# Pooled attention and an affine residual MLP on one core: the first batch's start put in another order

## Chip, core and metric

The kernel runs on one core of a Trainium2 chip. The metric is the device time of one execution in microseconds (us), lower is better. Before the change three executions took 361.34, 361.68 and 361.83 us, median 361.68. The profiled execution has a span of 360.4 us.

## What is computed

Two stages in one kernel. The first is attention over pooled keys and values: 8 batches, 8 heads, 576 tokens, 64 features a head. k and v are averaged over groups of 8 tokens, so that there are 72 keys a head. The second is a residual block: mixing over tokens with a 576x576 matrix, then a two-layer MLP with 2048 hidden columns. All inputs and the output are float32.

```python
k_p = k.reshape(B, H, Sp, 8, D).mean(axis=3)          # Sp = 72
v_p = v.reshape(B, H, Sp, 8, D).mean(axis=3)
attn = softmax(scale * q @ k_p^T)                      # over the 72 pooled keys
x = (attn @ v_p), heads side by side                   # (8, 576, 512)

a1 = alpha1 * x + beta1
tok = einsum('ts,bsd->btd', w_tok, a1)
u = x + lam * tok
a2 = alpha2 * u + beta2
ch = relu(a2 @ w_ch1) @ w_ch2
out = u + lam * ch
```

Setup work is done once in the kernel: `lam` and `lam * alpha1` are spread over 128 partitions (a product of a row of ones with the vector), w_tok is transposed and its row sums are appended, beta2's share is folded into a bias of the hidden columns, and w_ch2 is multiplied by lam.

## The kernel before

Each engine takes its instructions in program order. Tokens are split: rows 0 to 511 of a batch in a main part, rows 512 to 575 as the remainder ("rem"). Loads that change the type to 16 bits go through GpSimd's queue, the others through the sync or the scalar queue. The pieces of attention of one batch are functions which the program calls in an order of its own:

```python
def broadcast(i, out, by=None):                # vector i to all partitions
    ps = gp("ps_bc")
    nc.tensor.matmul(out=ps, lhsT=ones_row, rhs=vecs[0:1, i])      # float32
    if by is None:
        nc.scalar.copy(out=out, in_=ps)
    else:
        nc.vector.tensor_tensor(out=out, in0=by, in1=ps, op=ALU.mult)

def keep_warm(count):                          # products that nothing reads
    ps = psB.tile([P, DM], FP, tag="ch", bufs=2, name="ps_warm")
    for _ in range(count):
        nc.tensor.matmul(out=ps, lhsT=warm[:, 0:P], rhs=warm)

# att_F(b, hp): 4 transposes of q of two heads on TensorE, then a copy to qT
# att_Frem(b):  2 transposes of the remainder of q, then a copy
# att_K(b, u):  pools k of four heads on TensorE, copies to kpT (half on ScalarE, half on VectorE)
# first_V(b, u): pools v of four heads: 6 products, 2 copies
# att_S(b, h):  scores of a head (3 products), 2 exponentials on ScalarE -> ET
# att_AV(b, h): 5 products of ET with pooled v, reciprocal and normalisation on VectorE -> x
# att_X(b, h0, h1, eng): xs = x * lam * alpha1 for heads h0 to h1
# mix_T(b, c):  token mixing of one chunk of 128 tokens: 5 products, u = x + ..., u_bf = u * alpha2
# mix_uT(key):  4 transposes of u_bf, copy to u_fm on ScalarE
# setup_wtok(t): 5 transposes of w_tok's tile t, copy;  setup_rowsum(t): 5 products, copy
# setup_bias(g): 16 narrow products for the bias of 4 hidden tiles, copy
# mlp_A(n, j):  hidden tile j of block n: 4 products, activation -> Hj
# mlp_B(n, m, part): a quarter of the second layer for chunk m
# scale_w2(g):  w2[g] *= lam on VectorE (128 x 2048)
```

The PSUM tiles named `gp` share six buffers. The first batch is called in this order:

```python
new_batch(1)
keep_warm(2)
broadcast(1, lamal_bc)                         # alpha1
broadcast(0, lam_bc)                           # lam
keep_warm(1)
cast_rem(0, nc.vector)
bias_rows()                                    # two products beta1 * lam, one row each
att_F(0, 0)
att_F(0, 1)
att_Frem(0, nc.scalar.copy)
keep_warm(1)
att_K(0, 0, None)                              # its first lines copy k on VectorE
nc.vector.tensor_tensor(out=lamal_bc, in0=lamal_bc, in1=lam_bc, op=ALU.mult)
more_constants()
keep_warm(2)
att_S(0, 0)
att_S(0, 1)
# ... cut: att_F of heads 4 to 7, scores 2 to 5, second half of k, first half of v
att_AV(0, 0)
att_AV(0, 1)
# ... cut: the other heads, xs, tiles 0 to 3 of w_tok with their row sums
mix_T(0, 0, nc.gpsimd)
setup_rowsum(3)
mix_T(0, 1, nc.gpsimd)
# ... cut: loads of w1[3] and w2
mix_T(0, 2)
mix_T(0, 3)
mix_uT((0, 0))
mix_uT((0, 1))
setup_bias(0)
mlp_A(0, 0, 0, 256)
mix_uT((0, 2))
for j in range(1, 4):
    mlp_A(0, j, 0, 256)
mix_uT((0, 3))
for j in range(4):
    mlp_A(0, j, 256, 512)
```

After that a loop over 9 blocks of 512 tokens sorts the pieces by a number: hidden tile j of a block stands at j, the second layer from 16 on, and the attention of the next batch and the rest of the setup lie between.

```python
if n == 0:
    todo.append((4.6, lambda: setup_wtok(4, nc.scalar.copy)))
    todo.append((6.2, lambda: setup_rowsum(4)))
    todo.append((8.3, setup_wtok_odd))
    for g in range(1, 4):
        todo.append((4 * g - 0.8, lambda g=g: setup_bias(g)))
    for g in range(4):
        todo.append(((11.0, 11.2, 11.4, 16.6)[g], lambda g=g: scale_w2(g)))
```

Of the kernel before, what the change touches and what calls it, by code (L numbers as in the profile page):

```python
# [23 lines left out]
def kernel(  # L24
# [42 lines left out]
    def new_batch(b):  # L67
        st1[b] = {"qT": [None] * 2, "ET": [None] * H, "raw": [None] * 2, "q": [None] * 2,
                  "k": [None] * 2, "v": [None] * 2}
# [4 lines left out]
    def load_q_bf(b, u, behind=None):  # L74

        bf = work.tile([P, 4, 4, D], BF, tag="q_bf", bufs=4, name="q_bf")
        if behind is not None:
            behind.memset(bf[:, 0, 0, 0:1], 0.0)
        nc.gpsimd.dma_start(out=bf.rearrange("p h c d -> p h (c d)"), in_=rows(q, b, u))
        st1[b]["q"][u] = bf  # L80
# [36 lines left out]
    def load_rem(b, queue=nc.sync, behind=None):  # L117

        raw = work.tile([P, 2, 2, 2, D], FP, tag="rem_raw", bufs=2, name="rem_raw")
        if behind is not None:  # L120
            behind.memset(raw[:, :, :, 0, 0:1], 0.0)
        for i, src in enumerate((q, k)):
            for h in range(2):
                (nc.scalar if h and not b else queue).dma_start(
                    out=raw[:, i, h].rearrange("p c d -> p (c d)"),
                    in_=src[b, h::2, 512:576, :].rearrange("a (i c) d -> i a (c d)", c=2))
        st1[b]["rem_raw"] = raw
# [25 lines left out]
    def cast_rem_k(eng):  # L153
        raw, rk = st1[0]["rem_raw"], st1[0]["rem"][1]
        eng.tensor_copy(out=rk[:, :, 0:2], in_=raw[:, 1])
        eng.tensor_copy(out=rk[:, :, 2], in_=raw[:, 1, :, 0])
# [26 lines left out]
    ones_row = const.tile([1, P], FP, tag="ones_row", name="ones_row")  # L183
    nc.vector.memset(ones_row, 1.0)

    def load_vector(i, src):
        n = 65 if i in (0, 3) else 1
        nc.scalar.dma_start(out=vecs[0:n:64, i],
                            in_=src.unsqueeze(0).to_broadcast((1 + n // 65, DM)))

    new_batch(0)
    load_rem(0)
    load_q_bf(0, 0)
    load_k16(0, 0)
    load_vector(1, moe_alpha1)
    load_vector(0, moe_lam)
    start = const.tile([1, 2], FP, tag="start", name="start")
    nc.vector.memset(start, 0.0)
    nc.scalar.activation(out=start[:, 1:2], in_=start[:, 0:1], func=AF.Exp, bias=0.0, scale=1.0)
    load_vector(3, moe_beta1)  # L200
    nc.scalar.dma_start(out=b2row, in_=moe_beta2.rearrange("(c p) -> c p", p=P))
    warm = const.tile([P, DM], BF, tag="warm", name="warm")
    nc.vector.memset(warm, 0.0)
# [12 lines left out]
    each4 = pool_each.rearrange("p (g a) j -> p g a j", a=4)  # L216
    nc.gpsimd.affine_select(out=identity_bf, in_=identity_bf, compare_op=ALU.not_equal,
                            fill=1.0, base=0, pattern=[[-1, P]], channel_multiplier=1)
    load_q_bf(0, 1)
    nc.gpsimd.affine_select(out=identity, in_=identity, compare_op=ALU.not_equal,  # L220
                            fill=1.0, base=0, pattern=[[-1, P]], channel_multiplier=1)
    for t, n, width in ((pool_main, 64, 2),):
# [4 lines left out]
    nc.gpsimd.affine_select(out=each4, in_=each4, compare_op=ALU.not_equal, fill=0.125,  # L227
                            base=0, pattern=[[-16, 8], [-1, 4], [-4, 4]], channel_multiplier=1)
    load_k16(0, 1)
    load_v16(0)  # L230
    load_wtok()

    vp1_pool, kpT_pool, ET_pool = [], [], []
# [19 lines left out]
                            in1=pool_v[0:32, 1:16:2], op=ALU.add)  # L253
    nc.vector.tensor_reduce(out=pool_rem, in_=pool_each, op=ALU.max, axis=AX.X)

    def bias_rows():
        for i, p0 in ((0, 64), (1, 0)):
            nc.vector.tensor_tensor(out=xs_pool[i][p0:p0 + 1, 4, :], in0=vecs[p0:p0 + 1, 3],
                                    in1=vecs[p0:p0 + 1, 0], op=ALU.mult)

    b2c_bf = const.tile([P, 4], BF, tag="b2c_bf", name="b2c_bf")
    wtT = const.tile([P, 6, 640], BF, tag="wtT", name="wtT")
# [8 lines left out]
    def load_al2(behind):  # L271
        behind.memset(al2_bc[:, 0:1], 0.0)
        nc.sync.dma_start(out=al2_bc, in_=moe_alpha2.unsqueeze(0).to_broadcast((P, DM)))
# [102 lines left out]
    def att_Frem(b, copy=None):  # L376
# [11 lines left out]
                                identity=identity_bf)  # L388
        copy(out=st["rem_qT"], in_=ps_q[:, 0:256].rearrange("p (c t) -> p c t", c=2))

    def att_K(b, u, copy):

        st = st1[b]
        ps_kp = gp("ps_kp")
        kp = ps_kp[:, 0:4 * SPG].rearrange("p (h g) -> p h g", g=SPG)
        n, nr = (1, 1) if b else (4, 2)
        if not b:
            nc.vector.tensor_copy(out=st["k"][u][:, :, 4], in_=st["k"][u][:, :, 0])
            if u == 0:
                cast_rem_k(nc.vector)  # L400
        for h in range(4):
            for c in range(n):
                nc.tensor.matmul(  # L403
                    out=kp[:, h, 0:64],
                    lhsT=st["k"][u][:, h, c:c + 2].rearrange("p a d -> p (a d)"),
                    rhs=pool_main, start=(c == 0), stop=(c == n - 1))
        for hh in range(2):
            for c in range(nr):
                nc.tensor.matmul(  # L409
                    out=kp[:, hh:4:2, 64:72],  # L410
                    lhsT=st["rem"][1][:, hh, c:c + 2].rearrange("p a d -> p (a d)"),
                    rhs=pool_rem.rearrange("p (g u r) -> p u r g", r=2, u=2)[:, u],
                    start=(c == 0), stop=(c == nr - 1))
        for a in range(2):
            rows = slice(64 * a, 64 * a + 64)
            (copy or (nc.scalar.copy, nc.vector.tensor_copy)[a])(  # L416
                out=kpT_pool[u][rows, a], in_=kp[rows])
# [87 lines left out]
    def keep_warm(count):  # L505
# [4 lines that stand above are left out]
# [75 lines left out]


    new_batch(1)
    keep_warm(2)
    broadcast(1, lamal_bc)
    broadcast(0, lam_bc)  # L590
    keep_warm(1)
    cast_rem(0, nc.vector)
    bias_rows()
    att_F(0, 0)
    att_F(0, 1)
    att_Frem(0, nc.scalar.copy)
    keep_warm(1)
    att_K(0, 0, None)
    nc.vector.tensor_tensor(out=lamal_bc, in0=lamal_bc, in1=lam_bc, op=ALU.mult)
    more_constants()  # L600
    keep_warm(2)
    att_S(0, 0)
    att_S(0, 1)
    att_F(0, 2, nc.vector.tensor_copy)
    att_F(0, 3, nc.vector.tensor_copy)
    att_S(0, 2)
    keep_warm(1)
    att_K(0, 1, None)
    load_al2(nc.vector)
    att_S(0, 3)  # L610
    setup_vectors()
    keep_warm(1)
    att_S(0, 4)
    first_V(0, 0)
    att_S(0, 5)
    att_AV(0, 0)
    att_AV(0, 1)
    for g in range(2):
        load_w1(g)
    load_q_bf(1, 0)  # L620
    load_q_bf(1, 1)
    load_w1(2)
    att_X(0, 0, 2, nc.gpsimd)
    first_V(0, 1)
    att_S(0, 6)
    att_AV(0, 2)
    att_S(0, 7)
    att_AV(0, 3)
    load_rem(1, behind=nc.vector)
    att_X(0, 2, 4, nc.gpsimd)  # L630
    att_AV(0, 4)
    att_AV(0, 5)
    setup_wtok(0, nc.scalar.copy)
    att_X(0, 4, 6, nc.gpsimd)
    att_AV(0, 6)
    setup_wtok(1, nc.scalar.copy)
    att_AV(0, 7)
# [5 lines left out]
    setup_wtok(3, nc.scalar.copy)  # L643
    att_X(0, 6, 8)
    setup_rowsum(2)
    load_v16(1)
    keep_warm(1)
    mix_T(0, 0, nc.gpsimd)
    setup_rowsum(3)
    mix_T(0, 1, nc.gpsimd)  # L650
    load_w1(3)
    for g in range(3):
        load_w2(g)
    mix_T(0, 2)
    mix_T(0, 3)
    mix_uT((0, 0))
    mix_uT((0, 1))
    setup_bias(0)
    mlp_A(0, 0, 0, 256)
    mix_uT((0, 2))  # L660
    for j in range(1, 4):
        mlp_A(0, j, 0, 256)
    mix_uT((0, 3))
    for j in range(4):
        mlp_A(0, j, 256, 512)

# [52 lines left out]
    for n in range(NBLK):  # L719
        todo = []  # L720
        for j in range(0 if n else 4, NJ):
            todo.append((j, lambda j=j: mlp_A(n, j)))
        for m in range(4):
            for part in range(4):
                at = 16 + (4 * m + part if n else 4 * part + m)
                todo.append((at, lambda m=m, part=part: mlp_B(n, m, part)))
        if n == 0:
            todo.append((4.6, lambda: setup_wtok(4, nc.scalar.copy)))
            todo.append((6.2, lambda: setup_rowsum(4)))
            todo.append((8.3, setup_wtok_odd))  # L730
            for g in range(1, 4):
                todo.append((4 * g - 0.8, lambda g=g: setup_bias(g)))
            for g in range(4):
                todo.append(((11.0, 11.2, 11.4, 16.6)[g], lambda g=g: scale_w2(g)))
        b = n + 1
        if b < B:
            todo += attention(b)
            if b + 1 < B:
                new_batch(b + 1)
                gate = nc.vector if b == 1 else None  # L740
                for u in range(2):
                    at = 21.0 + 0.2 * u
                    todo.append((at, lambda b=b, u=u: load_k(b + 1, u, gate)))
                    at = {1: 21.0, 2: 7.2}.get(b, 0.4) + 0.1 * u
                    todo.append((at, lambda b=b, u=u: load_q_bf(
                        b + 1, u, nc.vector if b == 2 else None)))
                    at = 19.0 + 0.2 * u if b == 1 else 3.5 + 4.0 * u
                    todo.append((at, lambda b=b, u=u: load_v(b + 1, u, behind=gate)))
                todo.append((20.9, lambda b=b: load_rem(b + 1, behind=gate)))
        for _, do in sorted(todo, key=lambda x: x[0]):  # L750
            do()
# [30 lines left out]
```

The softmax here doesn't subtract the row's maximum and nothing guards it: scores larger than these inputs give would overflow.

## Time and profile before

| engine | busy us | share of the span |
|---|---|---|
| PE (TensorE products) | 345.3 | 96% |
| PEld (TensorE weight loads) | 186.7 | 52% |
| DVE (VectorE) | 209.5 | 58% |
| ACT (ScalarE) | 154.1 | 43% |
| POOL (GpSimd) | 86.6 | 24% |

DMA moved 44.58 MB. The profile's second part cuts the span into 40 slices of 9.0 us each; a digit there is the busy share of a slice in tenths, and 9 means 90% or more. Its fourth part, the chain of waits, goes back from the last instruction to what released it, and so on; it can also be read for a stretch alone, in order of time, where each piece has a start, a length and a name. The timeline lists instructions with start, length, engine, line and tile; idle time before an instruction and what ended it stand in brackets. `ps_` names are PSUM tiles. A busy PE is not PE at its peak.

### The profile page before, as it was taken

The page shows a single profiled execution, that of the slowest core. Times are in us where ns is not written, and L with a number is a line of the kernel's source. Part 1 is how long each engine was busy: PE and PEld are TensorE (multiplying, and loading weights), DVE is VectorE, ACT ScalarE, POOL GpSimd, SP SyncE. Part 2 cuts the span into 40 slices and gives each one's busy share as a digit, 9 for nine tenths or more (in the row PEclk, how much of TensorE's full clock was granted, in tenths as well). Part 3 has the DMA queues.
Part 4 walks back from the last instruction along what each step waited for, and adds up shares of the span by engine and source line. Part 5 has one row for each costly group of instructions (what it writes and reads, how often), then busy time and mean ns, then how long its engine had stood idle before and what let it go on. Part 6 is the DMA issues. An engine that isn't in the chain of part 4 may idle for free.

```text
span 360.4 us, 5916 instructions
## 1 busy us (share of the span) xinstructions
PE 345.3 (96%) x2229; PEld 186.7 (52%) x2229; DVE 209.5 (58%) x452; ACT 154.1 (43%) x319; POOL 86.6 (24%) x99
## 2 busy tenths in 40 slices
PE   4988999899999999999999999999999999999994
PEld 1566765445644564456445644564456445545541
DVE  6484347688773778576748787677567870011011
ACT  2572995027900890069006900592059204704700
POOL 8469407261117000620052006200510000000000
PEclk9999999999999999999999999999999999999999
DMA  8999920977949872987199729872910132011012
GB/s 122 200 215 261 216 43 3 185 189 203 162 118 225 155 125 64 244 159 126 53 206 190 130 62 215 175 131 60 224 58 0 40 78 75 0 58 60 1 58 58
DMA packets 65886, 44.58 MB, mean 124 GB/s; under 512 B 32377, under 2 KB 57021, under 8 KB 65858
## 3 DMA queue, kind: packets, MB, share of 16 engines
q1 hardware_dynamic: 50480, 33.30, 38.6%
q0 software_dynamic: 15072, 10.76, 20.9%
q8 instruction: 17, 0.28, 0.3%
q10 hardware_dynamic: 306, 0.14, 0.2%
q14 instruction: 11, 0.09, 0.1%
HBM read 38.30 MB, written 9.44 MB: 132 GB/s over the span
## 4 chain that ended last, share of the span: by engine, by line
PE 89%; DVE 4%; ACT 3%; DMA 2%; SPq 1%; issue 1%; ACTq 0%; DVEq 0%
PE ps_ch L573 33%; PE ps_h L555 32%; PE ps_tok L518 11%; PE ps_sc L450 4%; PE ps_av L470 2%; DVE x_tm L478 2%; PE ps_sc L453 1%; ACT Hj L560 1%; DMA vecs<-in_moe_alpha_dram 1%; PE ps_bc L278 1%; PE ps_kp L403 1%; DMA rem_qT<-rem_q 1%; SPq L363 1%; DVE w L339 1%; PE ps_q L368 1%
## 5 line engine op out<-in xcount | busy, mean ns | idle before, releaser
L560 ACT ACTIVATE Hj<-ps_h,bias_cols 128x512 bf16<-128x512 f32 x144 | 98.8, 690 | 150.8 <-PE ps_h L555 149.9
L555 PE MATMUL ps_h<-u_fm,w 128*128 128x512 bf16 (+1 forms) x592 | 138.1, 374 | 1.4 <-ACT u_fm L541 1.1
L573 PE MATMUL ps_ch<-w,Hj 128*128 128x512 bf16 x576 | 133.7, 379 | 0.0
L573 PEld LDWEIGHTS <-Hj 128*128 128x128 bf16 x576 | 54.7, 98 | 62.7 <-issue 1.6
L555 PEld LDWEIGHTS <-w 128*128 128x128 bf16 x592 | 63.3, 114 | 45.7 <-issue 2.6
L578 DVE TENSOR_TENSOR u_sb<-u_sb,ps_ch 128x512 f32<-128x512 f32 x36 | 24.5, 688 | 75.1 <-PE ps_ch L573 74.7
L518 PE MATMUL ps_tok<-xs,wtT 128*128 128x512 bf16 (+3 forms) x200 | 44.5, 380 | 1.8 <-DVE xs L485 1.8
L455 ACT ACTIVATE ET<-ps_sc 72x256 f16<-72x256 f32 (+1 forms) x128 | 44.8, 405 | 2.6 <-PE ps_sc L450 2.5
L522 DVE TENSOR_TENSOR u_sb<-x_tm,ps_tok 128x512 f32<-128x512 f32 (+1 forms) x40 | 27.5, 687 | 19.5 <-PE ps_tok L518 19.4
L478 DVE TENSOR_TENSOR x_tm<-ps_av,rec 128x320 f32<-128x320 f32 x64 | 31.5, 492 | 2.5
L147 POOL CAST rem_q<-rem_raw 128x256 bf16<-128x256 f32 x7 | 2.9, 421 | 123.0 <-DMA rem_raw<-in_q_dram 123.0
L518 PEld LDWEIGHTS <-wtT 128*128 128x128 bf16 (+3 forms) x200 | 17.3, 100 | 23.6 <-issue 1.8
L438 DVE TENSOR_TENSOR v_u<-v_u 72x512 f32<-72x512 f32 (+1 forms) x48 | 27.5, 573 | 1.2
L525 DVE TENSOR_TENSOR u_bf<-u_sb,al_bc 128x512 bf16<-128x512 f32 x34 | 26.3, 775 | 1.2
L450 PE MATMUL ps_sc<-qT,kpT 128*72 128x256 bf16 x128 | 25.4, 278 | 0.1
L476 DVE RECIPROCAL rec<-ps_av 128x5 f32<-128x5 f32 x64 | 12.3, 192 | 21.1 <-PE ps_av L474 20.2
L470 PEld LDWEIGHTS <-ET 72*128 72x128 f16 x256 | 16.0, 97 | 11.9 <-issue 0.5
L162 POOL TENSOR_TENSOR k_raw<-k_raw 128x512 f32<-128x512 f32 x14 | 18.2, 1303 | 14.1 <-DMA k_raw<-in_k_dram 13.6
L164 POOL TENSOR_TENSOR k_bf<-k_raw 128x512 bf16<-128x512 f32 x14 | 19.0, 1354 | 1.1
L485 DVE TENSOR_TENSOR xs<-x_tm,lamal_bc 128x512 bf16<-128x512 f32 x26 | 18.3, 704 | 0.9
L470 PE MATMUL ps_av<-vp,ET 72*128 72x66 f16 x256 | 18.0, 193 | 0.3 <-ACT wtT L299 0.3
L416 DVE CAST kpT<-ps_kp 64x288 bf16<-64x288 f32 x26 | 11.8, 455 | 10.5 <-PE ps_kp L409 5.2
(111 smaller groups left out, 217.5 us busy)
## 6 DMA issues: line engine op xcount, KB each, us to landing
out_dram<-u_sb SPq DMA_DIRECT2D x32, 256.0 KB
k_raw<-in_k_dram SPq DMA_DIRECT2D x14, 512.0 KB
v_u<-in_v_dram SPq DMA_DIRECT2D x12, 512.0 KB
q_bf<-in_q_dram POOLq DMA_DIRECT2D x16, 256.0 KB, 7.0
w<-in_moe_w_ch_dram POOLq DMA_DIRECT2D x8, 512.0 KB, 11.3
v<-in_v_dram POOLq DMA_DIRECT2D x4, 256.0 KB, 7.5
out_dram<-u_sb SPq DMA_DIRECT2D x8, 128.0 KB
rem_raw<-in_q_dram SPq DMA_DIRECT2D x15, 64.0 KB
```

The lines of the kernel that those rows point to most:

```text
L438: nc.vector.tensor_tensor(out=t[:, :, 0:n], in0=t[:, :, 0:n], in1=t[:, :, n:2 * n], op=ALU.add)
L450: nc.tensor.matmul(out=ps_sc[0:SPG, 0:256], lhsT=kpT_pool[u][:, half, h % 4, :], rhs=st["qT"][u][:, 2 * (h % 4):2 * (h % 4) + 2, :])
L455: nc.scalar.activation(out=ET[:, n0:n0 + n], in_=ps_sc[0:SPG, 0:n], func=AF.Exp, bias=0.0, scale=0.125)
L470: nc.tensor.matmul(out=av[:, odd + c, :], lhsT=ET[:, m0:m0 + 128], rhs=vp1[:, hh, :])
L478: nc.vector.tensor_tensor(out=x[:, 1 - odd:6 - odd, dd:dd + D], in0=av[:, :, 0:64], in1=rec.unsqueeze(2).to_broadcast((P, 5, D)), op=ALU.mult)
L518: nc.tensor.matmul(out=ps_tok[p0:p1], lhsT=wtT[0:kk, at, P * c:P * c + p1 - p0], rhs=xs_pool[i][0:kk, sc, :], start=(sc == 0), stop=(sc == 4))
L522: nc.vector.tensor_tensor(out=s["u"][p0:p1, :], in0=x[p0:p1, 1 + c if c < 4 else 5 - 5 * i, :], in1=ps_tok[p0:p1, 0:DM], op=ALU.add)
L525: eng.tensor_tensor(out=s["u_bf"], in0=s["u"], in1=al2_bc, op=ALU.mult)
L555: nc.tensor.matmul(out=ps_h[:, t0:t1], lhsT=w1_of(cc, j), rhs=u_fm[n][:, cc, t0:t1], start=(cc == 0), stop=(cc == 3))
L560: nc.scalar.activation(out=t, in_=ps_h, func=AF.Relu, bias=bias_cols[:, j:j + 1], scale=1.0)
L573: nc.tensor.matmul(out=ps, lhsT=Hj[n, j][:, 128 * m:128 * m + 128], rhs=w2[j // 4][:, j % 4, :], start=(j == 0), stop=(j == NJ - 1))
L578: nc.vector.tensor_tensor(out=u, in0=u, in1=ps, op=ALU.add)
```

## The change

The work of the kernel is nearly the same after the change; its order in the first batch is another. In the order of the diff:

- lambda's vector is loaded first on the scalar queue; alpha1 and beta1 go to the sync queue;
- on GpSimd's queue the first half of v (and its remainder) is loaded ahead of the second halves of k and q, and the second half of v after them. The last batch-0 loads and those of batch 1's v are split in the same way;
- alpha1 is broadcast later, and its product with lam is taken straight from PSUM;
- the doubled copies of k (`double_k`) are a function of their own, called ahead of other VectorE work; the two beta1 * lam products are separate (`bias_row`), one early, one in the loop;
- heads are interleaved differently: pooled v and outputs of the first heads come between the scores, before the second half of k;
- there are 11 unread products where there were 9;
- tile 4 of w_tok, row sum 3 and bias group 1 move ahead, to between the mixing products; the third scaling of w2 moves a little back.

It is meant to let the engines start on the first batch sooner and to put setup work into waits.

```diff
-    def load_vector(i, src):
+    def load_vector(i, src, queue=nc.scalar):
...
     new_batch(0)
+    load_vector(0, moe_lam)
     load_rem(0)
     load_q_bf(0, 0)
     load_k16(0, 0)
-    load_vector(1, moe_alpha1)
-    load_vector(0, moe_lam)
+    load_vector(1, moe_alpha1, nc.sync)
+    load_vector(3, moe_beta1, nc.sync)
...
-    load_vector(3, moe_beta1)
...
-    load_q_bf(0, 1)
+    load_v16(0, (0, 1))
...
     load_k16(0, 1)
-    load_v16(0)
+    load_q_bf(0, 1)
+    load_v16(0, (2,))
     load_wtok()
...
+    def double_k(u):
+        nc.vector.tensor_copy(out=st1[0]["k"][u][:, :, 4], in_=st1[0]["k"][u][:, :, 0])
+        if u == 0:
+            cast_rem_k(nc.vector)
...
     new_batch(1)
-    (the order shown above)
+    for g in range(2):
+        load_w1(g)
+    load_q_bf(1, 0)
+    load_q_bf(1, 1)
+    load_w1(2)
+    keep_warm(2)
+    broadcast(0, lam_bc)
+    keep_warm(2)
+    att_F(0, 0)
+    att_F(0, 1)
+    more_constants()
+    cast_rem(0, nc.vector)
+    att_Frem(0, nc.scalar.copy)
+    keep_warm(1)
+    double_k(0)
+    att_K(0, 0, None)
+    bias_row(0)
+    keep_warm(1)
+    att_S(0, 0)
+    att_S(0, 1)
+    first_V(0, 0)
+    att_S(0, 2)
+    double_k(1)
+    att_AV(0, 0)
+    att_S(0, 3)
+    keep_warm(1)
+    att_K(0, 1, None)
+    att_AV(0, 1)
+    broadcast(1, lamal_bc, lam_bc)
+    att_F(0, 2)
+    att_F(0, 3, nc.vector.tensor_copy)
+    att_X(0, 0, 2, nc.gpsimd)
+    att_AV(0, 2)
+    keep_warm(1)
+    att_S(0, 4)
+    first_V(0, 1)
+    att_AV(0, 3)
+    att_X(0, 2, 4, nc.gpsimd)
+    load_al2(nc.vector)
+    att_S(0, 5)
+    setup_vectors()
+    keep_warm(1)
+    att_AV(0, 4)
+    att_S(0, 6)
+    keep_warm(1)
+    att_AV(0, 5)
+    load_rem(1, behind=nc.vector)
+    att_X(0, 4, 6, nc.gpsimd)
     att_S(0, 7)
...
     setup_rowsum(2)
-    load_v16(1)
     keep_warm(1)
+    load_w1(3)
+    load_v16(1, (0, 1))
+    setup_rowsum(3)
     mix_T(0, 0, nc.gpsimd)
-    setup_rowsum(3)
     mix_T(0, 1, nc.gpsimd)
-    load_w1(3)
+    load_v16(1, (2,))
     for g in range(3):
         load_w2(g)
+    setup_bias(0)
     mix_T(0, 2)
+    mix_uT((0, 0))
     mix_T(0, 3)
-    mix_uT((0, 0))
+    setup_wtok(4, nc.scalar.copy)
     mix_uT((0, 1))
-    setup_bias(0)
+    setup_bias(1)
     mlp_A(0, 0, 0, 256)
     mix_uT((0, 2))
-    for j in range(1, 4):
-        mlp_A(0, j, 0, 256)
+    mlp_A(0, 1, 0, 256)
+    mlp_A(0, 2, 0, 256)
     mix_uT((0, 3))
+    mlp_A(0, 3, 0, 256)
...
-            todo.append((4.6, lambda: setup_wtok(4, nc.scalar.copy)))
+            todo.append((4.5, lambda: bias_row(1)))
...
-            for g in range(1, 4):
+            for g in range(2, 4):
...
-                todo.append(((11.0, 11.2, 11.4, 16.6)[g], lambda g=g: scale_w2(g)))
+                todo.append(((11.0, 11.2, 13.4, 16.6)[g], lambda g=g: scale_w2(g)))
```

More of the change, by code (lines that the diff above doesn't have):

```diff
@@ L184 @@
     nc.vector.memset(ones_row, 1.0)
-    def load_vector(i, src):
+    def load_vector(i, src, queue=nc.scalar):
         n = 65 if i in (0, 3) else 1
-        nc.scalar.dma_start(out=vecs[0:n:64, i],
-                            in_=src.unsqueeze(0).to_broadcast((1 + n // 65, DM)))
+        queue.dma_start(out=vecs[0:n:64, i],
+                        in_=src.unsqueeze(0).to_broadcast((1 + n // 65, DM)))
     new_batch(0)
+    load_vector(0, moe_lam)
     load_rem(0)
@@ L254, with bias_row @@
     nc.vector.tensor_reduce(out=pool_rem, in_=pool_each, op=ALU.max, axis=AX.X)
[L256 to L259, printed above, removed]
+    def bias_row(i):
+        p0 = 64 - 64 * i
+        nc.vector.tensor_tensor(out=xs_pool[i][p0:p0 + 1, 4, :], in0=vecs[p0:p0 + 1, 3],
+                                in1=vecs[p0:p0 + 1, 0], op=ALU.mult)
     b2c_bf = const.tile([P, 4], BF, tag="b2c_bf", name="b2c_bf")
@@ L396, in att_K @@
         n, nr = (1, 1) if b else (4, 2)
[L397 to L400, printed above, removed]
         for h in range(4):
@@ L587 @@
     new_batch(1)
[L588 to L617, printed above, removed]
     for g in range(2):
@@ L622 @@
     load_w1(2)
+    keep_warm(2)
[24 more added lines that the diff above has]
+    att_F(0, 3, nc.vector.tensor_copy)
     att_X(0, 0, 2, nc.gpsimd)
+    att_AV(0, 2)
+    keep_warm(1)
+    att_S(0, 4)
     first_V(0, 1)
+    att_AV(0, 3)
[5 more added lines that the diff above has]
+    att_AV(0, 4)
     att_S(0, 6)
-    att_AV(0, 2)
+    keep_warm(1)
+    att_AV(0, 5)
+    load_rem(1, behind=nc.vector)
+    att_X(0, 4, 6, nc.gpsimd)
     att_S(0, 7)
[L628 to L632, printed above, removed]
     setup_wtok(0, nc.scalar.copy)
-    att_X(0, 4, 6, nc.gpsimd)
     att_AV(0, 6)
```

## The prediction

> **What bounds the kernel now.** I read the busy row per slice first, then the chain of waits cut to the first 65 us, then the timeline of that stretch, then the waits of each engine in it. The page:
>
> ```profile
> PE   4988999899999999999999999999999999999994
> PEld 1566765445644564456445644564456445545541
> DVE  6484347688773778576748787677567870011011
> ACT  2572995027900890069006900592059204704700
> ...
> DMA  8999920977949872987199729872910132011012
> ```
>
> One slice is 9.0 us. From the fifth slice on, PE shows 9 everywhere but for one 8, up to the last slice: there TensorE sets the time and nothing in this change makes its work smaller. The room is in the first four slices (0 to 36 us). The change lives in that room and in its edge. In the chain of waits that is:
>
> ```profile
> 2.44 3.88 DMA vecs<-in_moe_alpha_dram
> 6.32 0.04 issue
> 6.36 3.77 PE ps_bc L278 x4
> 10.13 0.54 PE ps_warm L509
> 10.67 0.85 PE ps_q L368 x8
> ...
> 25.55 1.02 DVE xs L485
> 26.56 0.14 issue
> 26.70 1.24 PE ps_tok L518 x5
> ...
> 35.88 1.91 PE ps_h L555 x16
> ```
>
> Columns: start, length, what. TensorE sits until 6.36 for alpha's vector, which left third on its queue, then spends 3.77 us on two broadcasts. Only then does it touch q. Between 19.99 and 26.56 the chain is VectorE's: eight reciprocals and normalisations and the product xs. At 26.70 token mixing starts, at 35.88 the second halves of the first hidden columns, and from 39.87 to 47.28 the chain is nearly all ScalarE copies and activations. One more idle spot lies behind that, in the timeline:
>
> ```profile
> 44.03 4.73 DVE L339 TENSOR_TENSOR w<-w,lam_bc 128x2048 bf16<-128x2048 bf16 x2 [0.23 <-DMA w<-in_moe_w_ch_dram]
> 58.86 2.28 DVE L339 TENSOR_TENSOR w<-w,lam_bc 128x2048 bf16<-128x2048 bf16 x1
> 64.32 1.25 PE L518 MATMUL ps_tok<-xs,wtT 128*128 128x512 bf16 x5 [1.12 <-DVE xs L485]
> ```
>
> In brackets stands the idle time before an instruction and what ended it: TensorE waited 1.12 us for xs at 64.32, behind a 2.28 us scaling of w2 on VectorE; and the second scaling waited for its load, so w2 arrives just in time for VectorE.
>
> **What the Trainium skill says.** "TensorE: Matmul & The Clock Gate", section "What's actually happening": the array starts at half clock, and goes to full clock after about 3.4 us of sustained work, in a window that doesn't start with the kernel. The trace agrees in kind: two unread 512-column products take 0.87 us in the chain at 13.11 (0.43 each), while sixteen 256-column products take 1.91 at 35.88 (0.24 per 512 columns); eight transposes take 0.85 at 10.67 and 0.45 at 14.98. So full speed came only at about 14.5 us. The page's granted-clock row reads 9 throughout and doesn't show it. "DMA: Bandwidth & Descriptors", section "Issuing engines are not separate DMA queues": spreading loads over issuing engines saves only issue time. The trace has 0.52 to 0.69 us per vector issue on ScalarE's queue, and that is what moving alpha and beta to the sync queue frees. "SBUF — State Buffer", section "Who interferes with whom": a VectorE instruction with two SBUF inputs contends with a GpSimd instruction that reads SBUF. The trace agrees: VectorE's xs product takes 1.01 us at 25.55 beside GpSimd's, 0.71 at 63.56.
>
> **Part by part.**
>
> (a) Lambda first, alpha later. Lambda's load now leaves at about 0.80. Alpha took 3.88 us from issue to landing, so I put lambda at 4.7 (an estimate). One broadcast is half of 3.77, 1.89: 6.6. Two unread products at 0.43: 7.5. The first half of q needs its 6.4 us (the shortest of four landings in the tile view) from issue at 1.31: 7.7. Eight transposes 0.85: 8.6. Remainder transposes 0.21 and one unread product 0.43: 9.25. The first half of k lands at 2.22 + 6.6 = 8.8, and its three VectorE copies (0.21, 0.28, 0.21) end at 9.5, so pooling k (0.94) ends at about 10.3; before, 13.11. Copies of pooled k: 0.39 on ScalarE, then 0.46 on VectorE. First exponential at about 11.15, against 14.23: **3.1 us earlier**. The copies of k ahead of bias rows cost nothing; bias_rows' two products of 0.68 leave the front.
>
> (b) Loads by halves. GpSimd's loads land in order at a steady pace: the timeline shows it held for the landing of the second q at 10.66, second k at 12.00, first v at 13.34, so 1.34 us per 256 KB. With v's first half and its 64 KB rest moved third and fourth, they land at about 10.7 and 11.0, second k at 12.3, second q at 13.7, the last v at 15.0. No bytes are saved. Pooled v can now run right behind the first scores, so attention output of head 0 starts before the second half of k is even pooled.
>
> (c) The new order of heads. Following it instruction by instruction with the means of the table (exponentials 0.38 and 0.43 before overlap, 0.35 each in a row; reciprocal plus normalisation 0.65; copy of pooled v 0.24; copy of q 0.59), scores 0 to 2 run to 13.4 with VectorE's first normalisation at 14.1 (20.22 before). But then TensorE's own order takes over: second k (0.55), a late alpha broadcast (about 0.9 if the array is fast by then, 1.9 if not), transposes of the second q, their copy on ScalarE, and only then scores of head 4, at about 17.1; its exponentials 17.4 against 18.09. So **2.4 of the 3.1 us are lost again on ScalarE's side** in waits that the new order makes. The last exponential ends at about 21.1 against 22.45. VectorE, started six microseconds earlier, ends head 7 at 22.6 against 25.51, and xs at about 24.0 against 27.0.
>
> (d) Who ends last before mixing. Now ScalarE: after the exponentials it has four copies of transposed w_tok (0.69) and three row sums (0.26), 3.5 us in a row: 24.6. The fourth row sum (0.39) now stands ahead of mixing: mixing starts at about 24.9 against 26.70, **1.8 us earlier**.
>
> (e) Mixing to the first hidden columns. Four mixes at 1.08, bias 0 (0.51), two transposes of u (0.22), tile 4 of w_tok (0.24) and bias 1 (0.51) go on TensorE in between: 31.1; the copy of w_tok's tile 4 (0.50) is ahead of the second u copy (0.59) on ScalarE, so the first hidden product starts at 31.5 against 32.86: only 1.4 earlier, but 0.75 us of TensorE work has been done already that stood later. With the third and fourth u then, the second halves start at 34.1 against 35.88: 1.8.
>
> (f) What leaves the ScalarE-bound stretch. The copies for w_tok tile 4 (0.50) and bias 1 (0.20) leave 39.87 to 47.28. ScalarE is what ends there, so 0.7 us more: **2.5 us in all**.
>
> (g) What comes in. bias_row(1), 0.68 on VectorE while it waits (7.97 us idle before the first scaling of w2): free. The third scaling of w2 (2.3) moves from the idle stretch 46.4 to 48.8 to between heads 1 and 2 of the second batch, where VectorE has 0.65 of work per 1.32 us: it is late by about 1.5 us and catches up in three heads. Cost 0 to 0.4; I take 0.2. Two more unread products (11 for 9) at 0.2 to 0.4 lie in waits.
>
> Sum: 361.68 - 2.5 + 0.2 = 359.4; rounded down a little for full clock that may come sooner: **359.3 us**.
>
> **Rivals.** First, loading is the true bound: the DMA row shows 8 and 9 over 45 us and the windows show 191 to 287 GB/s from 6 to 46. If the whole shift only makes scaling of w2 or pooling of batch 1's k wait longer, nothing is left: 361 to 362. For it: VectorE waited 7.97 us for w2 already. Against: the first use of scaled w2 is at 56.93, ten microseconds after the last scaling, and the bytes in flight are those of before. Second, the order wins more than I follow: if the array is at full clock by 11 us rather than 14.5, late broadcast and transposes cost half, scores of head 4 move to 16.5, and ScalarE's tail with them: 358 or a little less. For it: more unread products and no gap from 4.7 on. Third, the interleaving binds tighter: VectorE has nearly no slack from 13 to 24 us, and TensorE waits in its order for each v copy or PSUM buffer (six shared); each 0.3 us wait over eight heads would eat the gain: 361 or slightly slower.
>
> **Range and chances.** The second rival with all of (a) kept would be 3.1 + 0.7, about 357.9; luck with both more; the first and third end at 361 to 362. I take 357.3 to 361.4 for 8 in 10. Two per cent is 7.2 us, more than twice what any path here gives: faster 0.04, within 0.95, slower 0.01.
>
> **What would show it.** In the changed trace: the broadcast of lambda starting near 4.7; first exponential near 11.2; head 4's exponentials near 17.4 (much earlier means rival two); mixing at 24.9, released by ScalarE's row sum rather than VectorE's xs; second halves at 34.1; at 47 us a lead of 2.5. Wrong would be: a lead of 2 us or more at 35 that is gone at 60 (rival one, seen as DMA waits of the w2 scalings or of the k sums), or waits of TensorE for v copies at 13 to 20 us (rival three).

## The result: no change, and the profile after

The changed kernel takes 361.86 us (median; 361.08 to 362.00), the kernel before in the same comparison 361.75 us. The ratio is 0.9999 with a 95% interval of 0.998 to 1.0017. The prediction was 359.3 us; the gain of 2.4 us that it promised did not come. Medians and ranges here are of all executions; a ratio leaves out those over 1.5% above the fastest of their kernel (one each of e6 and e8, three of e10).

It is not that nothing happened. The rows of the page for TensorE's busy share, its granted clock and the DMA, in tenths, 9.0 us a slice:

```profile
PE   7989997999999999999999999999999999999994
...
PEclk9999999899999999999999999999999999999999
DMA  8999930957948873886198729872710132011012
```

TensorE's first and fourth slices are fuller than before (7 and 9 for 4 and 8), and then it gets worse: TensorE falls to 7 in the seventh (54 to 63 us), and the granted clock shows an 8 in the eighth (63 to 72 us). The chain of waits of the changed kernel, in order of time (start, length, what; "issue" is time in which nothing is seen to be waited for), shows where the lead was won and lost. Its line numbers are up to 3 higher than those of the kernel before:

```profile
1.31 5.33 DMA q_bf<-in_q_dram
6.64 0.05 issue
6.69 1.03 PE ps_q L369 x8
...
24.46 2.17 PE ps_tok L521 x10
...
33.42 1.91 PE ps_h L558 x16
...
44.47 1.89 PE ps_h L558 x8
...
56.28 3.13 DVE w L340
...
62.59 0.82 PE ps_tok L521 x3
63.41 0.05 issue
63.47 0.46 PE ps_tok L521
63.92 3.34 PE ps_ch L576 x8
67.26 1.08 PE ps_tok L521 x5
```

The lines of the kernel before for the same work behind 40 us, from its chain:

```profile
47.33 1.89 PE ps_h L555 x8
...
58.95 2.20 DVE w L339
...
64.32 1.25 PE ps_tok L518 x5
65.57 1.73 PE ps_ch L573 x8
67.30 1.08 PE ps_tok L518 x5
```

Token mixing of batch 0 starts 2.24 us sooner (24.46 against 26.70), the second halves of the first hidden columns 2.46 us sooner (33.42 against 35.88), the hidden products that follow the ScalarE-bound stretch 2.86 us sooner (44.47 against 47.33). Then, within five microseconds, all of it goes. The first mixing of batch 1 starts only 1.73 us sooner (62.59), and the second mixing at 67.26 against 67.30: almost nothing is left. From there on the two kernels are alike.

Two things stand between 60 and 67 us. The timeline of TensorE says what they are. The columns are start, length, engine, line and tiles; the brackets give idle time and what ended it. The fourth line is of the kernel before:

```profile
58.45 1.89 PE L576 MATMUL ps_ch<-w,Hj 128*128 128x512 bf16 x8
62.59 1.33 PE L521 MATMUL ps_tok<-xs,wtT 128*128 128x512 bf16 x4 [2.26 <-DVE xs L488]
63.72 3.54 PE L576 MATMUL ps_ch<-w,Hj 128*128 128x512 bf16 x8
...
65.41 1.89 PE L573 MATMUL ps_ch<-w,Hj 128*128 128x512 bf16 x8
```

First, the wait for xs ahead of batch 1's first mixing is 2.26 us, where it was 1.12. Second, eight products that took 1.89 us before now take 3.54. A table of stages shows what went with it. Each line has the stage and its length, then the busy time and number of instructions of TensorE, its weight loads, VectorE, ScalarE and GpSimd, then the granted clock (1.00 is full), the DMA share and GB/s:

```profile
61.00:62.60 1.60, 0.01 (x1) 0.01 (x1) 1.47 (x5) 0.00 (x0) 1.52 (x3) 1.00 0.49 29
62.60:64.00 1.40, 1.35 (x5) 0.64 (x7) 0.37 (x5) 0.00 (x0) 0.90 (x2) 0.87 0.76 240
64.00:66.00 2.00, 2.00 (x6) 0.73 (x5) 1.34 (x2) 0.00 (x0) 0.00 (x0) 0.50 1.25 196
66.00:68.00 2.00, 2.00 (x9) 0.73 (x8) 0.00 (x0) 0.00 (x0) 0.00 (x0) 0.74 1.27 193
```

The clock is 1.00 while TensorE sits idle and 0.50 soon after it has started again. It stays at half for about 3.4 us (an estimate from the table: 1.40 x 0.13 + 2.00 x 0.50 + 2.00 x 0.26 is 1.70 us of clock lost, or 3.4 us at half). So the ledger is 2.86 won, 1.14 lost in a longer wait, 1.65 lost at half clock on the eight products; 0.07 remain. It is the ledger of one execution of each kernel.

### The profile page after: what moved, and what is told of

The parts are those of the page before. It is cut to its first block, busy times and chain, and to the rows that moved or that the text cites. A ratio compares the mean times of both kernels' runs of the same rounds, so it can differ in the third digit from the quotient of the medians.

```text
span 360.3 us, 5879 instructions
## 1 busy us (share of the span) xinstructions
PE 345.3 (96%) x2190; PEld 186.8 (52%) x2231; DVE 208.2 (58%) x451; ACT 154.3 (43%) x319; POOL 88.9 (25%) x99
## 4 chain that ended last, share of the span: by engine, by line
PE 89%; DVE 3%; ACT 3%; DMA 2%; issue 1%; SPq 0%; DVEq 0%; POOLq 0%
PE ps_ch L576 33%; PE ps_h L558 33%; PE ps_tok L521 11%; PE ps_sc L453 4%; PE ps_av L473 2%; DVE w L340 1%; DMA q_bf<-in_q_dram 1%; PE ps_sc L456 1%; DVE x_tm L481 1%; ACT wtT L300 1%; PE ps_kp L406 1%; DMA rem_qT<-rem_q 1%; PE ps_q L369 1%; PE ps_v L429 1%; ACT ET L458 0%
## 5 line engine op out<-in xcount | busy, mean ns | idle before, releaser
L525 DVE TENSOR_TENSOR u_sb<-x_tm,ps_tok 128x512 f32<-128x512 f32 (+1 forms) x40 | 27.5, 687 | 22.6 <-PE ps_tok L521 22.6
L481 DVE TENSOR_TENSOR x_tm<-ps_av,rec 128x320 f32<-128x320 f32 x64 | 31.5, 492 | 2.5
L521 PEld LDWEIGHTS <-wtT 128*128 128x128 bf16 (+3 forms) x200 | 17.4, 100 | 23.7 <-DVE xs L488 2.7
L441 DVE TENSOR_TENSOR v_u<-v_u 72x512 f32<-72x512 f32 (+1 forms) x48 | 26.5, 552 | 1.2
L164 POOL TENSOR_TENSOR k_bf<-k_raw 128x512 bf16<-128x512 f32 x14 | 18.1, 1294 | 1.1
L340 DVE TENSOR_TENSOR w<-w,lam_bc 128x2048 bf16<-128x2048 bf16 x4 | 10.1, 2521 | 12.1 <-DMA w<-in_moe_w_ch_dram 12.1
```

What stands on the lines that cost most here:

```text
L441: nc.vector.tensor_tensor(out=t[:, :, 0:n], in0=t[:, :, 0:n], in1=t[:, :, n:2 * n], op=ALU.add)
L481: nc.vector.tensor_tensor(out=x[:, 1 - odd:6 - odd, dd:dd + D], in0=av[:, :, 0:64], in1=rec.unsqueeze(2).to_broadcast((P, 5, D)), op=ALU.mult)
L521: nc.tensor.matmul(out=ps_tok[p0:p1], lhsT=wtT[0:kk, at, P * c:P * c + p1 - p0], rhs=xs_pool[i][0:kk, sc, :], start=(sc == 0), stop=(sc == 4))
L525: nc.vector.tensor_tensor(out=s["u"][p0:p1, :], in0=x[p0:p1, 1 + c if c < 4 else 5 - 5 * i, :], in1=ps_tok[p0:p1, 0:DM], op=ALU.add)
```

## Experiments

**Theory A** was this ledger: the longer wait is VectorE's, and the idle time brings on the half clock. **Rival B**: the loads or a later stage set the time whatever happens at 62 us; w2's first part did land later here, VectorE waited for it until 43.62 instead of 41.51. **Rival C**: the half clock has another cause than idle time. **Theory D**, a refinement: the third scaling of w2, which the change moved by a little, is what makes the wait long.

### Unread products in the wait (e1_fill)

```diff
+    def keep_warm_gp(count):
+        ps = gp("ps_fill")
+        for _ in range(count):
+            nc.tensor.matmul(out=ps, lhsT=warm[:, 0:P], rhs=warm)
...
+            todo.append((21.75, lambda: keep_warm_gp(8)))
```

> The changed kernel with eight more unread products on TensorE (0.216 us each, 1.7 us) just ahead of the first mixing product of batch 1, inside the 2.26 us wait for xs. Nothing else moves. Theory A (the lead of 2.9 us is lost in two parts: a longer wait for xs, then 3.4 us at half clock that this idle time brings on): the wait stays, the clock stays full, the eight ps_ch products behind it take 1.9 us instead of 3.5, and the kernel gains 1.65 us: about 360.2. Rival B (late loads or a later stage set the time whatever happens at 62 us): 361.5 to 362. Rival C (the half clock is a power limit and not brought on by idle time): clock still 0.5 near 65 us, 361.9.

The result is 359.93 us, ratio 0.9943 (0.9922 to 0.9964). TensorE's timeline in it:

```profile
59.42 1.89 PE L518 MATMUL ps_fill<-warm 128*128 128x512 bf16 x8
61.93 1.24 PE L527 MATMUL ps_tok<-xs,wtT 128*128 128x512 bf16 x5 [0.62 <-DVE xs L488]
63.01 1.89 PE L582 MATMUL ps_ch<-w,Hj 128*128 128x512 bf16 x8
```

Eight products that nobody reads make the kernel 1.9 us faster than the changed one. The xs wait isn't shorter (the fill only covers it), yet the eight ps_ch products are back to 1.89 us. The granted clock is 1.00 from 60 to 72 us. Rivals B and C fall: idle time brought the half clock, and what is saved at 62 us stays saved to the end. The loads that start near 62 us do not bring it either: they start here too (DMA share 0.96 from 62 to 64 us). In this execution TensorE came to its wait at 59.42, 0.92 us sooner than in the changed kernel's; such differences come back below.

### The fourth scaling out of the way (e2_scale3_late, and e4_before_scale3_late on the kernel before)

```diff
-                todo.append(((11.0, 11.2, 13.4, 16.6)[g], lambda g=g: scale_w2(g)))
+                todo.append(((11.0, 11.2, 13.4, 25.3)[g], lambda g=g: scale_w2(g)))
```

On the kernel before it was 11.0, 11.2, 11.4, 25.3.

> The changed kernel with the fourth scaling of w2 on VectorE moved from between heads 4 and 5 of batch 1 to behind the third mixing of batch 1 (place 25.3 instead of 16.6). Theory A: xs is ready about 3.2 us earlier, TensorE's wait of 2.26 us at 60.3 is nearly gone (0 to 0.4), so is the half clock: 361.9 - 2.0 - 1.65, about 358.2, with perhaps 0.3 back where the scaling now delays mixing. Rival B: 361.5 to 362. If only the wait counts and the clock drops elsewhere: 359.9.

> The kernel before with the fourth scaling of w2 moved to place 25.3 as in the run above. Theory A: its wait of 1.12 us ahead of the first mixing of batch 1 goes, there was no half clock to save: 360.6. The gap to the changed kernel with the same move is then the front's own gain, 2.4 to 2.9 us. Rival B: 361.7, no change, and no gap.

The result is 357.87 us for the changed kernel with this edit, ratio 0.9891 (0.9865 to 0.9917), and 360.58 us for the kernel before with it, ratio 0.9969 (0.9958 to 0.998). Both lie within 0.4 us of theory A. Mixing starts without a wait in the first:

```profile
58.59 1.89 PE L576 MATMUL ps_ch<-w,Hj 128*128 128x512 bf16 x8
60.42 1.25 PE L521 MATMUL ps_tok<-xs,wtT 128*128 128x512 bf16 x5
61.51 1.89 PE L576 MATMUL ps_ch<-w,Hj 128*128 128x512 bf16 x8
```

The gap between the two, 2.7 us, is what the rest of the change gains, with the third scaling's move still in it, and it lasts to the end once the spot at 60 us is clear of waiting.

### The third scaling put back (e3_scale2_back)

```diff
-                todo.append(((11.0, 11.2, 13.4, 16.6)[g], lambda g=g: scale_w2(g)))
+                todo.append(((11.0, 11.2, 11.4, 16.6)[g], lambda g=g: scale_w2(g)))
```

> The changed kernel with the third scaling of w2 put back to its old place, ahead of all heads of batch 1 (11.4 instead of 13.4). Theory D (the move of that scaling into the row of heads is what lets the fourth scaling start beside GpSimd's xs product and last 3.2 us instead of 2.3): the fourth takes 2.3 again, the wait for xs is 1.2 to 1.6 us, clock maybe full: 359.5 to 360.5. Theory A without D: w2's third part has landed only at about 48.5, head 0 waits for the scaling until 50.8, VectorE has caught up by head 4, and the wait for xs is 2 to 2.3 as before: 361.5 to 362.

The result is 358.40 us, ratio 0.99 (0.988 to 0.992). This was the surprise: putting one VectorE instruction back makes the changed kernel 3.5 us faster, more than the 1.4 to 2.4 us that were expected. The timeline of VectorE and GpSimd in the changed kernel:

```profile
51.98 2.28 DVE L340 TENSOR_TENSOR w<-w,lam_bc 128x2048 bf16<-128x2048 bf16 x1
56.20 3.22 DVE L340 TENSOR_TENSOR w<-w,lam_bc 128x2048 bf16<-128x2048 bf16 x1
...
52.14 3.25 POOL L488 TENSOR_TENSOR xs<-x_tm,lamal_bc 128x512 bf16<-128x512 f32 x1 [11.38 <-DVE x_tm L481]
56.00 1.27 POOL L488 TENSOR_TENSOR xs<-x_tm,lamal_bc 128x512 bf16<-128x512 f32 x1
57.35 2.39 POOL L492 TENSOR_TENSOR xs<-x_tm,lamal_bc 64x128 bf16<-64x128 f32 x1
```

The same with the third scaling back in its place:

```profile
56.36 2.28 DVE L340 TENSOR_TENSOR w<-w,lam_bc 128x2048 bf16<-128x2048 bf16 x1
...
52.50 1.27 POOL L488 TENSOR_TENSOR xs<-x_tm,lamal_bc 128x512 bf16<-128x512 f32 x1 [11.59 <-DVE x_tm L481]
55.20 1.26 POOL L488 TENSOR_TENSOR xs<-x_tm,lamal_bc 128x512 bf16<-128x512 f32 x1 [0.90 <-DVE x_tm L481]
56.55 2.41 POOL L492 TENSOR_TENSOR xs<-x_tm,lamal_bc 64x128 bf16<-64x128 f32 x1
...
61.82 1.25 PE L521 MATMUL ps_tok<-xs,wtT 128*128 128x512 bf16 x5 [1.13 <-DVE xs L488]
```

The fourth scaling starts at the same time in both (56.20 and 56.36): VectorE does catch up. But in the changed kernel GpSimd's product of heads 2 and 3 has started at 56.00, just ahead of it, and the scaling takes 3.22 us instead of 2.28; with the third scaling back, that product started at 55.20 and is over 0.1 us after the scaling starts. The engine that comes second loses nearly the whole overlap: GpSimd's product at 52.14 takes 3.25 us instead of 1.27 behind the third scaling, and that is what makes the next product late. The Trainium skill's statement ("SBUF — State Buffer", section "Who interferes with whom"), that a VectorE instruction with two SBUF inputs contends with a GpSimd one that reads SBUF, agrees with these lengths; the prediction cites it and did not apply it in this place. The scaling starts 0.16 us sooner and lasts 0.94 us longer, so xs and with it mixing come 0.77 us later (62.59 for 61.82). The other 0.36 us between the waits of 1.13 and 2.26 us is TensorE's own: it came to the wait that much later in e3's execution. The half clock follows the longer wait only. The later mixing and the half clock make up the 2.5 us between the two profiled executions (359.46 and 361.96); the rest of the 3.5 us between the medians isn't accounted for. Theory D holds; my figure for the alternative, that the third part of w2 lands too late for its old place, was wrong: in this run two scalings ran back to back from 44.40 to 49.13, and the first head came at 49.49.

### That one move on the kernel before (e5_before_scale2_moved)

```diff
-                todo.append(((11.0, 11.2, 11.4, 16.6)[g], lambda g=g: scale_w2(g)))
+                todo.append(((11.0, 11.2, 13.4, 16.6)[g], lambda g=g: scale_w2(g)))
```

> The kernel before with one thing of the change alone: the third scaling of w2 from place 11.4 to 13.4. Theory D, as the runs so far shaped it: the third scaling makes GpSimd's xs product of heads 2 and 3 late, the fourth scaling then meets it and lasts 3.2 us, the wait for xs ahead of batch 1's first mixing grows from 1.12 to about 2.2 us, and half clock follows for 3.4 us: 361.8 + 1.1 + 1.65, about 364.5. If the collision needs the changed front: 361.8. If the wait grows but the clock stays: 362.9.

The result is 363.35 us, ratio 1.0039 (1.0024 to 1.0054); the profiled execution 364.11. Its timeline has the same pattern:

```profile
59.03 3.22 DVE L339 TENSOR_TENSOR w<-w,lam_bc 128x2048 bf16<-128x2048 bf16 x1
...
58.83 1.27 POOL L485 TENSOR_TENSOR xs<-x_tm,lamal_bc 128x512 bf16<-128x512 f32 x1
...
65.42 1.46 PE L518 MATMUL ps_tok<-xs,wtT 128*128 128x512 bf16 x3 [2.26 <-DVE xs L485]
```

One number in the sorted list, 13.4 for 11.4, costs an otherwise untouched kernel 1.4 us, through the same collision, the same 3.22 us and the same wait of 2.26 us. Here TensorE's front is that of the kernel before (second halves at 35.88 in both), and the scaling explains the wait alone: it starts 0.17 us later, lasts 0.94 us longer, and mixing comes 1.10 us later. In the profiled execution, the slowest of the four, the clock is at half for 3.4 us from 65.3 on. The other three took 363.15 to 363.50, nearer to the 362.9 of a longer wait alone. So the half clock probably doesn't follow in every execution here; the trace of only one was seen.

### The early broadcast alone (e6_before_lam_first)

```diff
     new_batch(0)
+    load_vector(0, moe_lam)
     load_rem(0)
...
+    load_vector(1, moe_alpha1, nc.sync)
+    load_vector(3, moe_beta1, nc.sync)
...
-    broadcast(1, lamal_bc)
     broadcast(0, lam_bc)
...
     att_F(0, 2, nc.vector.tensor_copy)
     att_F(0, 3, nc.vector.tensor_copy)
+    broadcast(1, lamal_bc, lam_bc)
```

The product of lamal_bc with lam_bc that stood behind the first pooling of k is gone, as in the change.

> The kernel before with part (a) of the prediction alone: lambda's vector first on the scalar queue, alpha and beta on the sync queue, one broadcast ahead of q's transposes, alpha's broadcast with its product from PSUM only after the transposes of heads 4 to 7. Order of heads, of loads on GpSimd's queue and of the setup stays. If the front's gain is that of the early start: the first exponential comes 2.9 us sooner, about 0.9 to 1.9 us go back for the late alpha broadcast, and the lead at the first hidden products is 1 to 2 us: 359.8 to 360.8. If the new order of heads and loads is needed for it (v's first half lands at 13.3 to 14 us, VectorE's row of heads stays as long): 361.2 to 361.8.

The result is 360.41 us, ratio 0.997 (0.9944 to 0.9995), executions from 359.12 to 364.74. In the profiled one (359.69) the second halves start at 34.13, 1.75 us sooner than in the kernel before, where the changed kernel has 2.46. How much of the gain the early broadcast makes alone is not settled by that: e10 below has the same early broadcast, and its trace has 35.16, only 0.72 us sooner. The median gains 1.5 us, the ratio 1.1. The wide spread is new; the next run suggests its kind.

### Without the unread products (e8_no_unread)

The kernel of e2_scale3_late with nine of its eleven unread products left out; no output depends on them.

```diff
     keep_warm(2)
     broadcast(0, lam_bc)
-    keep_warm(2)
     att_F(0, 0)
     att_F(0, 1)
...
-    keep_warm(1)                  (seven times, to the first mixing)
```

> The changed kernel with the fourth scaling at 25.3, and all unread products but the first two left out (9 of 11; nothing reads them, so the output stays the reference's). If they bring full clock sooner (about 12.5 us in the changed kernel's trace): without them full clock comes at 14 to 18 us, and 0.5 to 1.5 us are lost: 358.5 to 359.4. If they only fill waits: 357.9, or 0.2 to 0.5 less where they stood on TensorE's path.

The result is 361.76 us, ratio 0.9969 (0.9946 to 0.9993), executions from 357.83 to 363.21. With them it was 357.87, and 358.5 to 359.4 was expected. The profiled execution took 362.29, and TensorE's timeline in it reads:

```profile
11.14 1.02 PE L429 MATMUL ps_v<-v,pool_v 128*72 128x256 f16 x4
19.09 1.02 PE L429 MATMUL ps_v<-v,pool_v 128*72 128x256 f16 x4
22.75 0.62 PE L453 MATMUL ps_sc<-qT,kpT 128*72 128x256 bf16 x2
26.94 0.39 PE L309 MATMUL ps_rs<-wtT,ones_bf 128*128 128x128 bf16 x4
```

Four products of pooled v take 1.02 us at 11.14 and again at 19.09, two scores 0.62 us at 22.75; the first row sums at full speed (0.39) come at 26.94. In the changed kernel the array reached full speed near 12.4 us: there pairs of scores took 0.41 us from 12.80 on. The second halves of the hidden columns came at 37.28, 3.7 us later than in e2_scale3_late. So these nine unread products are worth 3.9 us in the median. Executions of 357.83 to 359.43 stand beside others of 361.29 to 363.21: the first band fits a full clock that comes early, the second the profiled one, but only one was seen in a trace.

### Both scalings moved (e7_both_scales), and more unread products (e9_more_unread)

```diff
-                todo.append(((11.0, 11.2, 13.4, 16.6)[g], lambda g=g: scale_w2(g)))
+                todo.append(((11.0, 11.2, 11.4, 25.3)[g], lambda g=g: scale_w2(g)))
```

and for the second run also

```diff
-    keep_warm(2)
+    keep_warm(3)
     broadcast(0, lam_bc)
-    keep_warm(2)
+    keep_warm(4)
```

> The changed kernel with both: third scaling back at 11.4, fourth at 25.3. Theory A with D: with the fourth out of the row of heads there is no wait left at 60 us, so the third's place matters no more: 357.9, as with the fourth moved alone. If the third scaling also costs TensorE something in the row of heads: 357.0 to 357.5.

> The changed kernel with both scalings moved as in the run of 357.07 us, and three more unread products at the very start: 3 for 2 ahead of lambda's broadcast, 4 for 2 behind it, in waits of 0.4 and 0.8 us for lambda and q. If unread products buy an earlier full clock: it comes 1 to 3 us sooner in more executions, and the median falls to 356.3 to 356.9. If the two behind lambda were enough: 357.0. If they only stand in the way (0.43 us each at half clock): 357.2 to 357.6.

The result is 357.07 us for e7, ratio 0.9862 (0.9847 to 0.9877): this version beats both kernels, by 1.4% against the one before. Against e2 (0.9865 to 0.9917) the intervals overlap, so whether the third scaling's place matters once the fourth is away stays open. In e7's trace the second halves of the hidden columns already start at 32.71, against 33.57 in e2's, and neither scaling has been reached there; full clock came sooner (four products of pooled v take 0.60 us at 11.24, and 1.02 at 11.51 in the changed kernel's). Kernels with the same front differ by up to 1.1 us at this point from trace to trace (32.67 in e1, 33.42 in the changed kernel, 33.80 in e3), so a lead read from one trace is good to about 1 us. Against e4, which has both scalings in the same places, e7 is 3.5 us faster (3.9 by the two ratios): that is what the rest of the change gains. e9 took 357.07 us too, ratio 0.9871 (0.9852 to 0.989): full speed came sooner in its trace (the 16 products that pool k take 0.82 us at 8.55, and 1.14 at 8.47 in the changed kernel's), but the time didn't follow.

### The old order of heads and loads (e10_old_order)

The kernel of e6 with three unread products for one behind lambda's broadcast, and the fourth scaling at 25.3. Against e7 it leaves out the new order of heads, the loads by halves, the copies of k ahead, and the setup work in waits; the unread products are as many but stand elsewhere.

> The kernel before with part (a) (lambda first, alpha late), two more unread products behind the broadcast of lambda (3 for 1), and the fourth scaling of w2 at 25.3; the old order of heads, loads and setup work. Against the changed kernel with both scalings moved (357.07) it leaves out only the new order of heads, loads by halves and setup work in waits. If these are worth what the leads at 47 us say (2.86 in the changed kernel, 1.77 with lambda first alone): 357.07 + 1.1, about 358.2, with a small spread. If the unread products were what was missing and the order is worth nothing: 357.1. If the old order's clock still comes late in some executions: a spread of 2 us or more, median 359 to 360.

The result is 359.62 us, ratio 0.9945 (0.9924 to 0.9966), executions from 357.82 to 363.76: of the three outcomes expected, the one with a wide spread. So those parts together are worth about 2.5 us in the median (3.0 by the two ratios), and much of the steadiness. One line of TensorE's timeline shows a part of it:

```profile
9.86 0.87 PE L403 MATMUL ps_kp<-pool_main,k 128*128 128x64 bf16 x13 [1.30 <-DVE k L398]
```

Here pooling k waits 1.30 us for VectorE's copy of k, which stands behind the two bias rows, and these wait for beta's vector, now late on the sync queue. In the changed kernel the copies are ahead of the bias rows. How the rest divides between loads, order of heads and setup wasn't tried.

## Why the prediction was wrong

**(a) Lambda first: right in kind, the estimate too large.** I put lambda's landing at 4.7 us, by alpha's 3.88 us from issue to landing. Its broadcast started at 2.85, so it landed about 2.0 us after its issue at 0.81. It was first on its queue, where alpha had been third. TensorE then waited 0.80 us for q (6.69, where I had 7.7). First exponential: 10.65, said 11.15.

**(b), (c) Order of heads: right.** Head 4's exponentials at 17.17 (said 17.4); head 7 normalised at 22.1 (said 22.6), xs complete at 23.3 (said 24.0). ScalarE, and no longer VectorE, ends last before mixing, as said.

**(d), (e), (f) Mixing and hidden columns: right.** 24.46 for 24.9, 30.82 for 31.5, 33.42 for 34.1; lead at 44.47 of 2.86 for 2.5.

**(g) What comes in: this step failed.** "Cost 0 to 0.4; I take 0.2" for the third scaling between heads. It is right that VectorE catches up. I did not ask what the delay does to GpSimd, whose xs products wait for the same heads and share access with VectorE. The product of heads 2 and 3 came to run beside the fourth scaling, which lasted 3.22 us for 2.28. The term measured 1.14 us in the wait for xs (2.26 against 1.12), and 1.65 us at half clock on top: 2.8 in place of 0.2. With 2.79 for that term and 2.86 for the lead the sum is 361.75 - 2.86 + 2.79 = 361.68, against 361.86 measured. I had the clock gate in hand and used it for the first 14 us only; and I had seen the wait of 1.12 us at 64.32 as "one more idle spot" without asking what would make it longer.

In the same step "two more unread products ... lie in waits" treats them as nothing but filling. e8, without nine of them, is 3.9 us slower in the median; what the two more are worth alone wasn't tried.

**The rivals.** The first (loads are the bound) had its sign, a lead at 35 us gone at 60 to 67 and longer DMA waits of w2's scalings, and yet was not the cause: with the same loads e2 and e3 keep the lead. (Its gap of "ten microseconds" is 8.2: the third scaling ends at 48.76, w2 is first used at 56.93.) None of the three named a clock that falls back.

## What to carry to other kernels

When a change gives one stage a lead, look at the next place where the bounding engine waits for another, and check there which instructions will now run beside each other: one VectorE instruction, moved in a list, brought two others on VectorE and GpSimd into a collision. A wait of TensorE is not only its own length; where it reached 2.26 us it cost 1.65 us more at half clock, and unread products in it gave that back (e1), while work taken out of the producer's way gave back both (e2). Before giving up a change that measured as zero, follow the lead stage by stage: here 2.9 us were there, and two numbers in a list made 357.07 us of 361.86. And take more than one trace before reading a microsecond of lead: here traces of the same front differed by 1.1.

## What the hardware showed

Idle time of 2.26 us on TensorE was enough for half clock in two traces (the changed kernel, e5), 1.1 us was not (in the traces of the kernel before and of e3 the clock stays at 1.00). The half clock lasted some 3.4 us both times but did not begin at a fixed distance from the wait: about 1.0 us after work had resumed in the changed kernel (63.6 against 62.59), and 0.1 us before it in e5 (65.3 against 65.42). In the 3.4 us ahead of the fall TensorE had been idle for 2.3 and 2.1 us. So the same wait, falling otherwise, may bring no half clock; three executions of e5 look like that, but none of them was seen in a trace. The Trainium skill's page "TensorE: Matmul & The Clock Gate", section "What's actually happening", has 3.4 us for the window and asks for at least a whole idle one; here about two thirds of the 3.4 us ahead of the fall were idle. The profile's clock column shows this fall as 0.50, but reads 1.00 in the first 26 us of e8, where the products' lengths say half speed; the start of a kernel has to be read from the products.

GpSimd and VectorE, each with two operands in SBUF, did not slow each other evenly: the one that started second took longer by nearly the whole overlap (VectorE's scaling 3.22 for 2.28, GpSimd's product 3.25 for 1.27).
